# Where a load at the layer changes is placed: by loads of lead on both sides, in place of the longest idle

## The chip, the cores and the metric

The kernel runs on one NeuronCore of a Trainium2 chip. The metric is the time of one execution on the device in microseconds (us); less is better. Three runs of the kernel before took 2502.89, 2504.6 and 2510.55 us, median 2504.6.

## The reference

Two layers, each a grouped-query attention block on a cached context and then a token-mixing MLP, for two sequences with one new token each:

```python
x = A_x
x = x + _A_ref(_layernorm(x), A_k_cache, A_v_cache, A_wq, A_wo)
x = x + _B_ref(_layernorm(x), B_w1, B_b1, B_w2, B_b2)
# ... and both once more, with the same caches and weights
```

`_A_ref` makes 32 query heads from x, takes softmax(q k / sqrt(128)) v against 8 key and value heads of 32768 positions by 128, and projects back with wo. `_B_ref` normalises over the 512 channels, widens the one token to 1792 with gelu, and narrows it again. Everything is float32, and each layer reads the whole cache again: 268 MB of keys and 268 MB of values.

## The kernel before

**Units and chunks.** A unit is one (layer, sequence, key head): 2 x 2 x 8 = 32 of them, numbered 0 to 31 by the list `units`. A unit has 8 chunks of keys and 8 of values, each of 4096 positions: 2 MB, 16 KB in each of the 128 partitions. "K16 c5" below is chunk 5 of the keys of unit 16, "V15 c4" chunk 4 of the values of unit 15. For a K chunk TensorE makes scores (`k_chunk`, line 413), for a V chunk it adds weights times values (`v_chunk`, line 555). The second layer of a sequence can only begin when its first is done, so the order of units is bent at three places, N1 = 13, N2 = 16 and N3 = 18: there the last unit of one layer runs into the first of the next, and the mixer runs between. Of head 7 (the keeper), some chunks stay on the chip from layer 0 to layer 1 and aren't loaded again: three K chunks (`KEPT_K`, in cells 0, 1 and 9) and seven V chunks in whole or in part (`KEPT`, in cells 6, 2, 11, 13, 3, 4, 5 for chunks 1 to 7).

**Steps.** All chunks of K and V stand in one list, `stream`, in the order in which TensorE takes them. A step t is a place in that list, counted in chunks; it runs from 0 to 511. The loop at the end of the kernel walks through the list: for each entry it issues the load and then the matmuls. All loads of K, V and weights are issued by SyncE (SP) on one queue, in this order (line 139); SP waits at each until the place it goes to has been read for the last time. Since SP isn't held up by TensorE otherwise, it runs ahead of the matmuls as far as free places allow, and so many loads stand in the queue.

**Places.** `mem` is one tile of SBUF: cells 0 to 8 of 2 MB form the ring for chunks, cells 9 to 12 are for weights (9 and 11 also take chunks), and behind them is a rest where part of V c4 stays. A half cell is 1 MB: "7.0" and "7.5" are the halves of cell 7. Away from the changes, loads are of 2 or 4 chunks and take cells in turn (`buffer`). At the changes (units 13 to 19, steps 216 to 311) they are of one chunk and go through `spread`, which returns one whole cell or two halves, or, for the rest of a partly kept V chunk, through `half`.

**The books of the planner**, all in Python, at build time:

- `busy`: for each half cell, the step by which its content has been read; for a whole cell the first half counts half a step earlier.
- `loaded`: chunks' worth of loads issued so far; `seen[t]`: that number at step t.
- `lead(k)`: the loads issued since the last use of place k. It says how much stands in the queue between the moment the place comes free and the load that goes there.
- `booked`: for each half cell, the steps at which a kept chunk will be loaded to it.
- `closed`: for cells 6 to 9, the step from which something else has them.

In the kernel before, `half` takes the half cell that has been idle longest among those that `clear` allows: no booked load between now and 1.5 steps after the last use. `spread` takes, of the whole cells with a lead of 2 or more that `clear` allows, the one idle longest; if there is none, two halves from `half`.

The kept V chunks of unit 16 are loaded in a changed order: `SOONER` loads V16 c1 (to cell 6) right before K16 c6 at step 259, and V16 c3 (to cell 11) before K17 c0 at step 263. For V15 c4 and V18 c4, two blocks that were kept in PSUM are copied by VectorE to the place of the chunk's rest (line 503), and the last eighth of a chunk is loaded.

Of the kernel before, what the change touches and what calls it, by code (L numbers as in the profile page):

```python
# [14 lines left out]
CK = 4096  # L15
JT = CK // P
# [8 lines left out]
KEPT_K = {0: 0, 1: 1, 2: 9}  # L25
KEPT = {1: (8, 6), 2: (4, 2), 3: (8, 11), 4: (5, 13), 5: (8, 3), 6: (8, 4), 7: (8, 5)}
# [10 lines left out]
QT = 4  # L37
# [7 lines left out]
def gqa_mixer_kernel(ctx: ExitStack, tc: tile.TileContext, x, kt, v, wqo, cols, out):  # L45
# [54 lines left out]
    WCELL0, WCELLS = RING * RING, 4  # L100
# [3 lines left out]
    mem = const.tile([P, (WCELL0 + WCELLS) * CK + REST * QT * DH], F32, name="mem")  # L104

    def cells(k, m=1):
        return mem[:, k * CK : (k + m) * CK]
# [9 lines left out]
        nc.sync.dma_start(cells(cell), wqo[h])  # L117


    HB = CK // 2  # L120
    busy = [0] * 2 * (WCELL0 + WCELLS + 1)
    now = [0]
    loaded, seen = [0], {0: 0}

    def hold(k, m, until):
        for j in range(2 * k, 2 * (k + m)):
            busy[j] = max(busy[j], until - 0.5 * (m == 1 and j == 2 * k))

    def idle(k, m=1):

        return max(busy[2 * k : 2 * (k + m)])

    def lead(k, m=1):

        t = idle(k, m)
        return loaded[0] - seen[-(-t // 1)] + (-t) % 1

    def load(t, src):
        nc.sync.dma_start(t, src)  # L139
# [2 lines left out]
    def buffer(m, limit, until):  # L142

        ks = range(0, limit - m + 1, m) if limit != EVEN else [k + j for k in PAIRS for j in range(0, 2, m)]
        k = min(ks, key=lambda k: idle(k, m))
        assert idle(k, m) <= now[0]
        hold(k, m, until)
        return cells(k, m)

    def half(until):  # L150

        k = min((j for j in range(2 * WCELL0) if clear(j, until)), key=lambda j: busy[j])
        assert busy[k] <= now[0]
        busy[k] = until
        return mem[:, k * HB : (k + 1) * HB]

    def clear(k, until):

        return until <= closed.get(k // 2, until) and all(r <= now[0] or r >= until + 1.5 for r in booked.get(k, ()))

    def spread(until):

        whole = [k for k in (*range(WCELL0 + 1), KEPT[3][1]) if idle(k) <= now[0] and lead(k) >= 2 and clear(2 * k, until) and clear(2 * k + 1, until)]
        if whole:
            k = min(whole, key=idle)
            hold(k, 1, until)
            return [cells(k)]
        return [half(until - 0.5), half(until)]
# [6 lines left out]
    booked, closed = {}, {}  # L175
# [134 lines left out]
    def unit_of(n):  # L310

        return units[n]
# [67 lines left out]
    def load_k(n, c, m, limit):  # L380
        layer, b, h = unit_of(n)
        stay = h == keeper and c in KEPT_K
        own = KEPT_K[c] if stay else None
        until = k_done[n, c + m - 1]
        if own is not None:
            if stay and not layer:
                until = k_done[units.index((1, b, h)), c + m - 1]
            hold(own, m, until)
            bufs = [cells(own, m)]
        elif limit == RING:  # L390
            bufs = spread(until)
        else:
            bufs = [buffer(m, limit, until)]
        src, f = piece(kt, b * HKV + h, c, m), 0
        for t in bufs:
            if not (stay and layer):
                load(t, src[:, f : f + t.shape[-1]])
            f += t.shape[-1]
        at = [q for t in bufs for q in quads(t)]
        for j in range(m):  # L400
            k_at[n, c + j] = at[j * (JT // QT) : (j + 1) * (JT // QT)]

    def k_chunk(n, c):

        kc = k_at.pop((n, c))
        half, i = divmod(c, PACK)
        if i == 0:
            sc_ps[n, half] = pscore.tile([P, 512], F32, name="scores")
        for k in range(SUB):
            at = R * (SUB * i + k)  # L410
            q = qpad[n % 2][:, 28 - at : 60 - at]
            for g in range(NG):
                nc.tensor.matmul(  # L413
                    sc_ps[n, half][32 * g : 32 * g + 32, :],
                    q,
                    kc[k * NG + g],
                    start=(i == 0 and k == 0),
                    stop=(i == PACK - 1 and k == SUB - 1),
                )
        if i == PACK - 1:  # L420
            if half == 0:
                mx[n] = field(n, 0, HALVES)
            nc.vector.tensor_reduce(mx[n][:, half : half + 1], sc_ps[n, half], axis=AX.X, op=ALU.max)  # L423
# [20 lines left out]
    def turn_scores(n, half):  # L444
        nc.vector.transpose(S[half], sc_ps[n, half])  # L445
# [27 lines left out]
    def stays(n, c):  # L473

        quads, cell = KEPT.get(c, (0, 0)) if unit_of(n)[2] == keeper else (0, 0)
        return quads, mem[:, cell * CK : cell * CK + quads * QT * DH]

    def load_v(n, c, m, limit):
# [7 lines left out]
        if stay:  # L486
            if layer == 0:
                load(own, src[:, :f])
                for j in range(2 if stay > QT else 1):
                    busy[2 * KEPT[c][1] + j] = v_done[units.index((1, b, h)), c]  # L490
            if stay == JT // QT:
                v_at[n, c] = at
                return
            bufs = [half(until)[:, : CK - f]]
        elif limit == RING:
            bufs = spread(until)
        else:
            bufs = [buffer(m, limit, until)]
# [319 lines left out]
    for n in range(NU):  # L818
        stream += [(n * NCH + c + m - 1, 0, n, c, m, limit) for c, m, limit in parts(n, 0)]
        for c, m, limit in parts(n, 1):  # L820
            if n in (N1, N2):
                key = (n + 1) * NCH + 1 + (c + 1) / (2 * NCH)
            elif n in (N1 + 1, N2 + 1):
                key = (n + 1) * NCH - 0.5 + max(c / (2 * NCH) - 0.5, c - ASIDE + 1)
            else:
                key = (n + 1) * NCH + c + m - 1 + (LAG if N1 < n <= N3 else 0)
# [1 line left out]
    stream.sort()  # L828


    kbeg, k_done, vbeg, v_done, t = {}, {}, {}, {}, 0
    for _, is_v, n, c, m, _ in stream:
        (vbeg if is_v else kbeg).setdefault(n, t)
        for j in range(m):
            t += 1
            (v_done if is_v else k_done)[n, c + j] = t
# [9 lines left out]
    for n in range(NU):  # L846
        layer, b, h = unit_of(n)
        kend, vend = k_done[n, NCH - 1], v_done[n, NCH - 1]
        ahead = v_done[n - 1, NCH - 1] if n else 0
# [52 lines left out]
        if units[n] == lay[layer, b][-1]:  # L902
            key = (layer, b)
# [53 lines left out]
    t = 0  # L957
# [69 lines left out]
```

## Time and profile before

| | |
|---|---|
| median of three runs | 2504.6 us (2502.89 to 2510.55) |
| the profiled execution | 2504.29 us, of which the span of its instructions is 2502.5 us |
| TensorE matmuls, weight loads | busy 1391.0 us (56%), 376.7 us (15%) |
| VectorE, ScalarE, GpSimd | busy 222.8, 185.3, 4.9 us |
| read from HBM | 1063.81 MB |
| mean granted TensorE clock | 0.774 |

How to read the views of the profile: a row of the timeline has start, duration, engine and line, what it writes and reads, the count, and in brackets the idle time before it and who ended it. In a row of the windows view the last three numbers are the granted TensorE clock, the busy share of the 16 DMA engines and GB/s. A row of the chain (the work that ended last, followed back from the end) has start, duration and what; a DMA in it lasts from its issue to its landing, so it contains the time for which it stood in the queue. "SPq" is an instruction of SP's queue.

### The profile page before, as it was taken

How to read it: one execution, taken by the hardware profiler on the slowest of the kernel's cores; microseconds unless marked ns; L12 is line 12 of the kernel's file. 1: busy time of each engine (PE TensorE's matmuls, PEld its weight loads, DVE VectorE, ACT ScalarE, POOL GpSimd, SP SyncE). 2: the span in 40 equal slices, each digit the busy share in tenths (PEclk: the TensorE clock that was granted, in tenths of full speed). 3: DMA queues.
4: the chain of work that ended last, by engine and by line, in shares of the span. 5: the costliest groups of instructions: out<-in, count | busy, mean ns of one | idle time of the engine just before them, and what ended most of it. 6: DMA issues, size and time to landing. Idle time of an engine off the chain costs nothing.

```text
span 2502.5 us, 20559 instructions
## 1 busy us (share of the span) xinstructions
PE 1391.0 (56%) x9326; PEld 376.7 (15%) x9326; DVE 222.8 (9%) x610; ACT 185.3 (7%) x550; POOL 4.9 (0%) x17
## 2 busy tenths in 40 slices
PE   4545554645445544667667875455546555455546
PEld 1111111111111111111111211111111111111112
DVE  0000000000000000001111110000000000010002
ACT  0000000000000000001002010000000000012002
POOL 0000000000000000000000000000000000000000
PEclk8777777777777777878888888677777677777878
DMA  9999999999999999999999999999999999999996
GB/s 419 434 434 432 435 429 434 431 435 432 431 430 431 433 432 432 428 425 413 426 381 423 423 431 433 430 432 433 433 430 432 433 436 432 430 435 428 432 433 288
DMA packets 34368, 1065.14 MB, mean 426 GB/s; under 512 B 4069, under 2 KB 4073, under 8 KB 4970
## 3 DMA queue, kind: packets, MB, share of 16 engines
q1 hardware_dynamic: 33992, 1063.80, 98.9%
q8 instruction: 73, 1.20, 0.2%
q14 instruction: 13, 0.11, 0.0%
q10 hardware_dynamic: 290, 0.04, 0.0%
HBM read 1063.81 MB, written 0.00 MB: 425 GB/s over the span
## 4 chain that ended last, share of the span: by engine, by line
DMA 72%; PE 26%; DVE 1%; issue 0%; ACT 0%; SPq 0%; POOL 0%; ACTq 0%; DVEq 0%
DMA mem<-in_v_dram 36%; DMA mem<-in_kt_dram 36%; PE scores L413 12%; PE acc L555 11%; PE kept L337 1%; PE rows L235 1%; PE bcast L337 1%; PE small L592 0%; PE small L349 0%; PE small L439 0%; ACT S L777 0%; PE small L584 0%; PE bcast L789 0%; PE kept L734 0%; SPq L139 0%
## 5 line engine op out<-in xcount | busy, mean ns | idle before, releaser
L413 PE MATMUL scores<-mem,small_sb 128*32 128x512 f32 x4096 | 637.1, 735 | 603.6 <-DMA mem<-in_kt_dram 602.9
L555 PE MATMUL acc<-mem,S 128*16 128x512 f32 x4088 | 608.4, 731 | 451.3 <-DMA mem<-in_v_dram 442.6
L413 PEld LDWEIGHTS scores<-mem,small_sb 128*32 128x32 f32 x4096 | 152.6, 128 | 987.5 <-issue 906.3
L450 ACT ACTIVATE S<-S,small_sb 128x128 f32<-128x128 f32 x240 | 123.4, 518 | 2101.9 <-DVE small_sb L441 1632.4
L555 PEld LDWEIGHTS acc<-mem,S 128*16 128x16 f32 x4088 | 134.0, 110 | 808.3 <-issue 682.0
L423 DVE TENSOR_REDUCE small_sb<-scores 128x1 f32<-128x512 f32 x64 | 44.3, 691 | 882.0 <-PE scores L413 882.0
L445 DVE STREAM_TRANSPOSE S<-scores 128x512 f32<-128x512 f32 x64 | 45.5, 710 | 126.2 <-PE acc L555 126.2
L337 PE MATMUL kept<-mem,small_sb 128*2 128x512 f32 x104 | 51.6, 622 | 1.7 <-DVE small_sb L263 1.7
L235 PE MATMUL rows<-mem,small_sb 128*1 128x512 f32 (+1 forms) x276 | 48.9, 621 | 3.1 <-ACT mem L777 2.4
L450 ACT ACTIVATION_READ_ACCUMULATOR S<-S,small_sb 128x1 f32 x240 | 44.8, 187 | 0.0
L435 DVE TENSOR_REDUCE small_sb<-small 1x4 f32<-1x128 f32 x32 | 8.8, 276 | 284.2 <-PE small L433 284.2
L525 DVE SCALAR_TENSOR_TENSOR S<-acc,small_sb,S 128x128 f32<-128x128 f32 x93 | 32.6, 351 | 3.3
L586 DVE RECIPROCAL small_sb<-small 128x4 f32<-128x4 f32 x32 | 5.9, 185 | 280.8 <-PE small L584 280.8
L594 DVE TENSOR_TENSOR small_sb<-small,small_sb 128x4 f32<-128x4 f32 x31 | 5.1, 164 | 284.8 <-PE small L592 284.8
L777 ACT ACTIVATE S<-bcast,small_sb 128x512 f32<-128x512 f32 x28 | 20.7, 775 | 97.7 <-DVE small_sb L646 83.9
L235 PE MATMUL rows<-S,small_sb 128*1 128x512 f32 (+1 forms) x56 | 21.1, 592 | 8.0 <-ACT S L777 8.0
L349 PE MATMUL small<-small_sb,mem 2*128 2x2 f32 x112 | 15.1, 252 | 17.9 <-DVE mem L346 17.9
L523 DVE TENSOR_SCALAR S<-acc,small_sb 128x128 f32<-128x128 f32 x31 | 10.9, 350 | 139.1 <-PE acc L555 139.1
L592 PEld LDWEIGHTS small<-small_sb,S 128*128 128x128 f32 x62 | 12.5, 252 | 49.1 <-issue 38.9
L337 PE MATMUL bcast<-mem,small_sb 128*1 128x512 f32 (+1 forms) x40 | 18.5, 592 | 1.2 <-DVE small_sb L306 1.2
L349 PEld LDWEIGHTS small<-small_sb,mem 2*128 2x128 f32 x112 | 13.9, 191 | 30.8 <-DVE mem L346 27.6
L592 PE MATMUL small<-small_sb,S 128*128 128x4 f32 x62 | 15.2, 316 | 5.0 <-DVE S L525 5.0
(132 smaller groups left out, 270.5 us busy)
## 6 DMA issues: line engine op xcount, KB each, us to landing
mem<-in_kt_dram SPq DMA_DIRECT2D x35, 2048.0 KB, 17.5
mem<-in_v_dram SPq DMA_DIRECT2D x20, 2048.0 KB, 15.7
mem<-in_v_dram SPq DMA_DIRECT2D x9, 4096.0 KB, 29.1
mem<-in_v_dram SPq DMA_DIRECT2D x29, 1024.0 KB, 10.6
mem<-in_wqo_dram SPq DMA_DIRECT2D x14, 2048.0 KB, 33.4
mem<-in_kt_dram SPq DMA_DIRECT2D x7, 4096.0 KB, 25.5
mem<-in_kt_dram SPq DMA_DIRECT2D x18, 1024.0 KB, 8.9
mem<-in_v_dram SPq DMA_DIRECT2D x2, 1280.0 KB, 15.4
```

The costliest lines, as they stand in the source:

```text
L235: nc.tensor.matmul(rows[32 * g : 32 * g + b + 1, :], weights if b else weights[:, 1:], row, start=False, stop=True, skip_group_check=True,)
L337: nc.tensor.matmul(q_ps[n][:m, :], xnT[:, d, b : b + m], wq_at(h)[:, d, :], start=(d == 0), stop=(d == DT - 1),)
L349: nc.tensor.matmul(pt[:, r * m : (r + 1) * m], q_row[n][:m, r * DH : (r + 1) * DH], ident[:m, :m], start=True, stop=True,)
L413: nc.tensor.matmul(sc_ps[n, half][32 * g : 32 * g + 32, :], q, kc[k * NG + g], start=(i == 0 and k == 0), stop=(i == PACK - 1 and k == SUB ...
L423: nc.vector.tensor_reduce(mx[n][:, half : half + 1], sc_ps[n, half], axis=AX.X, op=ALU.max)
L445: nc.vector.transpose(S[half], sc_ps[n, half])
L450: nc.scalar.activation(s[:, :, h], s[:, :, h], AF.Exp, bias=neg[n][:, h : h + 1], scale=SCALE, accum_out=lsum[n][:, half, h : h + 1],)
L523: nc.vector.tensor_scalar_mul(t, acc[:, :DH], mask[:, 0:1])
L525: nc.vector.scalar_tensor_tensor(t, acc[:, k * DH : (k + 1) * DH], mask[:, k : k + 1], t, op0=ALU.mult, op1=ALU.add)
L555: nc.tensor.matmul(acc[32 * g : 32 * g + R * QT, :], S[half][:, col : col + R * QT], vc[q], start=(c == 0 and q < NG), stop=(c == NCH - 1 ...
L592: nc.tensor.matmul(po[:, :R], asb, selh, start=True, stop=True)
L777: nc.scalar.activation(hid[key, f], px[key], AF.Gelu_apprx_tanh, bias=shift[key][:, f : f + 1], scale=slope[key][:, f : f + 1],)
```

## The change

A place now has a mark, `fit`, from which both `half` and `spread` choose. It is the least of: the lead of the place; for each booked load that is still to come, the loads between the new content's last use and that step (`between`, from a new list `brings` that holds for each step what it brings, so that kept chunks count nothing); 4; and 0 where the place is closed too early. A place still in use has lead 0. The highest mark wins, and among equal ones the longest idle. `spread` takes a whole cell if its mark is 2 or more, and else two halves. `clear` is gone. `hold` and `idle` take half cells too.

```diff
     def lead(k, m=1):
         t = idle(k, m)
-        return loaded[0] - seen[-(-t // 1)] + (-t) % 1
+        return loaded[0] - seen[-(-t // 1)] + (-t) % 1 if t <= now[0] else 0
...
     def half(until):
-        k = min((j for j in range(2 * WCELL0) if clear(j, until)), key=lambda j: busy[j])
-        assert busy[k] <= now[0]
-        busy[k] = until
-        return mem[:, k * HB : (k + 1) * HB]
-
-    def clear(k, until):
-        return until <= closed.get(k // 2, until) and all(r <= now[0] or r >= until + 1.5 for r in booked.get(k, ()))
+        k = min((k / 2 for k in range(2 * WCELL0)), key=lambda k: (-fit(k, 0.5, until), idle(k, 0.5)))
+        assert fit(k, 0.5, until) >= 1
+        hold(k, 0.5, until)
+        return mem[:, int(k * CK) :][:, : CK // 2]
+
+    def fit(k, m, until):
+        ahead = [between(until, r) for j in range(int(2 * k), int(2 * (k + m))) for r in booked.get(j, ()) if r > now[0]]
+        return min(4, lead(k, m), *ahead, 0 if until > closed.get(int(k), until) else 4)
+
+    def between(a, b):
+        return sum(brings[int(-(-a // 1)) : b])

     def spread(until):
-        whole = [k for k in (*range(WCELL0 + 1), KEPT[3][1]) if idle(k) <= now[0] and lead(k) >= 2 and clear(2 * k, until) and clear(2 * k + 1, until)]
-        if whole:
-            k = min(whole, key=idle)
+        k = min((*range(WCELL0 + 1), KEPT[3][1]), key=lambda k: (-fit(k, 1, until), idle(k)))
+        if fit(k, 1, until) >= 2:
             hold(k, 1, until)
             return [cells(k)]
         return [half(until - 0.5), half(until)]
...
-    kbeg, k_done, vbeg, v_done, t = {}, {}, {}, {}, 0
+    kbeg, k_done, vbeg, v_done, brings, t = {}, {}, {}, {}, [], 0
     for _, is_v, n, c, m, _ in stream:
+        kept_k = unit_of(n)[2] == keeper and c in KEPT_K
+        brings += m * [1 - (stays(n, c)[0] / (JT // QT) if is_v else kept_k) * unit_of(n)[0]]
```

More of the change, by code (lines that the diff above doesn't have):

```diff
@@ L117, in load_weights @@
         nc.sync.dma_start(cells(cell), wqo[h])
-    HB = CK // 2
     busy = [0] * 2 * (WCELL0 + WCELLS + 1)
@@ L125, in hold @@
     def hold(k, m, until):
-        for j in range(2 * k, 2 * (k + m)):
+        for j in range(int(2 * k), int(2 * (k + m))):
             busy[j] = max(busy[j], until - 0.5 * (m == 1 and j == 2 * k))
     def idle(k, m=1):
-        return max(busy[2 * k : 2 * (k + m)])
+        return max(busy[int(2 * k) : int(2 * (k + m))])
     def lead(k, m=1):
         t = idle(k, m)
-        return loaded[0] - seen[-(-t // 1)] + (-t) % 1
+        return loaded[0] - seen[-(-t // 1)] + (-t) % 1 if t <= now[0] else 0
     def load(t, src):
```

## Prediction

> **What bounds the kernel now.** I read the page first, then the windows around the changes, then the chain and SP's timeline where the windows show a hole. From the page:
>
> ```profile
> span 2502.5 us, 20559 instructions
> ...
> q1 hardware_dynamic: 33992, 1063.80, 98.9%
> ...
> DMA 72%; PE 26%; DVE 1%; issue 0%; ACT 0%; SPq 0%; POOL 0%; ACTq 0%; DVEq 0%
> ```
>
> The loads' packets take 98.9% of what sixteen DMA engines have in the span: the kernel is bound by loading, and the change moves no byte. So it can only win what the queue stands idle, and only lose by letting it stand idle elsewhere. Where does it stand idle? Windows (the last two columns are DMA share and GB/s):
>
> ```profile
> 1100.00:1130.00 30.00, 20.11 (x124) 4.08 (x118) 3.72 (x11) 5.78 (x18) 0.00 (x0) 0.83 1.01 427
> ...
> 1250.00:1265.00 15.00, 10.25 (x72) 2.69 (x72) 1.14 (x4) 4.15 (x16) 0.00 (x0) 0.77 1.01 429
> 1265.00:1270.00 5.00, 2.20 (x24) 0.35 (x12) 1.89 (x3) 0.00 (x0) 0.00 (x0) 1.00 0.97 408
> 1270.00:1275.00 5.00, 4.24 (x24) 1.35 (x28) 0.00 (x0) 0.00 (x0) 0.00 (x0) 0.66 0.69 280
> 1275.00:1280.00 5.00, 5.00 (x34) 1.29 (x27) 0.00 (x0) 0.00 (x0) 0.00 (x0) 1.00 0.27 61
> 1280.00:1285.00 5.00, 3.90 (x27) 1.51 (x25) 1.46 (x3) 0.00 (x0) 0.00 (x0) 1.00 0.87 367
> 1285.00:1310.00 25.00, 13.89 (x92) 3.52 (x96) 1.29 (x4) 0.29 (x1) 0.00 (x0) 0.73 1.01 429
> 1360.00:1390.00 30.00, 25.00 (x142) 6.97 (x142) 6.47 (x15) 7.74 (x10) 0.55 (x1) 0.94 1.01 420
> 1430.00:1460.00 30.00, 20.22 (x126) 4.40 (x126) 2.42 (x8) 4.15 (x16) 0.00 (x0) 0.80 1.01 427
> 1460.00:1490.00 30.00, 22.19 (x156) 6.12 (x160) 3.49 (x7) 0.00 (x0) 0.00 (x0) 0.83 1.02 430
> ```
>
> There is one hole in the stretch. Against 429 GB/s it costs 5 us times (1-408/429) + (1-280/429) + (1-61/429) + (1-367/429), that is 0.24 + 1.74 + 4.29 + 0.72 = **7.0 us**. What opens it stands in SP's timeline and the chain:
>
> ```profile
> 1256.62 8.40 SPq L139 DMA_DIRECT2D mem<-in_kt_dram  x3
> 1265.53 13.51 SPq L139 DMA_DIRECT2D mem<-in_v_dram  x2
> 1279.13 0.86 SPq L139 DMA_DIRECT2D mem<-in_kt_dram  x2
> ```
>
> ```profile
> 1198.78 15.30 DMA mem<-in_v_dram
> ...
> 1216.10 17.57 DMA mem<-in_kt_dram
> ...
> 1237.38 10.96 DMA mem<-in_kt_dram
> ...
> 1256.62 14.01 DMA mem<-in_kt_dram
> ...
> 1277.77 0.92 PE scores L413 x3
> ...
> 1278.71 0.33 SPq L139
> ...
> 1279.13 11.61 DMA mem<-in_kt_dram
> ```
>
> The three K issues from 1256.62 are K16 c4 and the two halves of c5; the two V issues are V15 c4's rest (1265.53) and V16 c1, which goes at 1278.71, released by scores. V16 c1 belongs in cell 6, and the code before put the first half of K16 c5 into 6.0, two chunks earlier: it lands, is multiplied, and only then may V16 c1 be issued, with an eighth of a load between.
>
> Two constants follow. V14 c6 lands at 1198.78 + 15.30 = 1214.08 and K16 c1, seven loads later, at 1237.38 + 10.96 = 1248.34: **4.89 us a load**. From an empty queue V16 c1 and K16 c6 landed 1278.71 to 1279.13 + 11.61 = 1290.74, 12.03 us for two: a start of **2.25 us**, so a lone load needs 7.14 from issue to landing, a half 4.7.
>
> **The change part by part.** I applied the new mark by hand to each placement from step 216 to 311, with the busy steps of the code before. As a sample, K16 c5 at step 257: 251.5 loads are issued. 6.0 has lead 2.5, but until its booked load at 259 there comes only V15 c4's eighth: mark 0.125. 7.0 was last used at 253.5, when 250 had been issued: 1.5 + 0.5, mark 2. 7.0 wins, then 7.5 with 1.5. The places that differ (before, then after):
>
> | step, load | before | after |
> |---|---|---|
> | 220, 222: rests of V13 c2, c4 | 4.0, 5.0 | 5.0, 2.5 |
> | 257: K16 c5 | 6.0 + 7.0 | 7.0 + 7.5 |
> | 258: V15 c4 rest | 7.5 | 2.0 |
> | 259, 261: K16 c6, c7 | 2, 8 | 8, 7 |
> | 263, 265: K17 c0, c1 | 7, 2 | 2, 8 |
> | 268 to 299: cells 7 and 8 | as in the kernel before | exchanged |
> | 303, 305: K19 c4, c5 | 8, 1 | 1, 0.0 + 0.5 |
> | 306: V18 c4 rest | 0.0 | 2.0 |
> | 307: K19 c6 | 2 | 2.5 + 1.0 |
>
> *Steps 220, 222.* A wait goes, hidden as the first window shows (share 1.01). SP's waits from 1000 to 1600 us:
>
> ```profile
> SPq L139 <- DVE kept L514: 11.0, 2, 9.7
> ```
>
> The 9.7 us are V13 c7, to cell 5, behind the copy out of 5.0. It is then released by step 220, but the queue was full: **0**. What hides it are the loads in front; without them up to 9.7 us would show.
>
> *Steps 257 to 265.* TensorE in that stretch:
>
> ```profile
> 1261.86 1.91 PE L555 MATMUL acc<-mem,S 128*16 128x512 f32 x16
> 1263.58 1.90 PE L413 MATMUL scores<-mem,small_sb 128*32 128x512 f32 x16
> 1265.30 1.90 PE L555 MATMUL acc<-mem,S 128*16 128x512 f32 x16
> 1270.76 3.15 PE L413 MATMUL scores<-mem,small_sb 128*32 128x512 f32 x16 [3.56 <-DMA mem<-in_kt_dram]
> ...
> 1277.21 2.28 PE L413 MATMUL scores<-mem,small_sb 128*32 128x512 f32 x13
> ```
>
> These are steps 252 to 255 and most of 257. Now K16 c5's halves wait for step 253 (by 1265.5), V15 c4's rest for step 254, whose last matmul ends 1267.20 (a wait that is added; behind it on SP stands V16 c1, which needs step 252 alone). So V16 c1 is issued by about 1267.6 instead of 1278.71. K16 c4 landed at 1256.62 + 14.01 = 1270.63; c5 follows at 1275.5, the rest, an eighth, at 1276.1, and V16 c1 at **1281.0** instead of 1290.74 - 4.89 = 1285.85. The queue doesn't run dry. What is late next: K16 c6 waits for step 255 (1273.91) and must go by 1285.9 - 7.14 = 1278.8, 4.9 us to spare; K16 c7 for step 257 (1279.5) and must go by 1290.8 - 7.14 = 1283.7, 4.2 to spare.
>
> So the last engine's landing gains 1285.85 - 1281.0 = 4.8 us, and the bytes gain 7.0. They differ since engines run dry at different times: in the DMA view of 1256 to 1296, in slices of 1 us, the rate falls over five slices before it is 0:
>
> ```profile
> GB/s 459 377 434 434 401 426 475 385 475 410 410 410 410 401 434 383 305 193 86 41 0 0 0 262 98 426 492 344 475 459 360 492 426 377 508 377 426 508 311 475
> ```
>
> The engines that were ahead lose that lead in the hole; whether it counts at the end depends on whether it would be there without the hole. I take the middle, **-5.9**, ends -4.8 and -7.0. The Trainium skill (DMA: Bandwidth & Descriptors, section "Why a DMA increments its semaphore by 16 and not by 1") says that the engines of a transfer finish independently and that only the full count means landed; the five falling slices agree, and by that rule alone one would take the 4.8.
>
> *Cells 7 and 8 exchanged*: the same waits under other names, 0.
>
> *Steps 303 to 309.* Here waits get longer, since cells 6 to 9 are closed and the mark shrinks from 3.5 to 2.5 (c4) and to 2 and 1.5 (c5). SP, TensorE, and a row of the chain:
>
> ```profile
> 1449.09 6.19 SPq L139 DMA_DIRECT2D mem<-in_kt_dram  x2
> ...
> 1469.48 9.29 SPq L139 DMA_DIRECT2D mem<-in_kt_dram  x3
> ```
>
> ```profile
> 1451.73 3.18 PE L555 MATMUL acc<-mem,S 128*16 128x512 f32 x16 [2.40 <-ACT S L450]
> ...
> 1460.14 1.92 PE L413 MATMUL scores<-mem,small_sb 128*32 128x512 f32 x16 [0.65 <-DMA mem<-in_kt_dram]
> 1461.88 1.04 PE L555 MATMUL acc<-mem,S 128*16 128x512 f32 x8
> 1467.52 1.91 PE L555 MATMUL acc<-mem,S 128*16 128x512 f32 x8 [4.60 <-DMA mem<-in_v_dram]
> 1472.50 3.64 PE L413 MATMUL scores<-mem,small_sb 128*32 128x512 f32 x16 [3.08 <-DMA mem<-in_kt_dram]
> 1475.88 2.03 PE L555 MATMUL acc<-mem,S 128*16 128x512 f32 x16
> ```
>
> ```profile
> 1449.09 23.27 DMA mem<-in_kt_dram
> ```
>
> The PE rows are steps 298, 301, 302 (in two halves), 303, 304. K19 c4, issued at 1449.09, now waits for step 298, 1454.91; it lands at 1472.36, so it may go as late as 1465. c5's halves wait for step 301 (by 1462.1) instead of 1454.96; they land at 1474.8 and 1477.3 and must go 4.7 before. V18 c4's rest waits for the first half of step 302 (1462.9). c6's first half waits for the second half of step 302 (1469.43, must go by 1475.7), its second half for 1.0 in step 303: 1474.3 by its first half, 1476.14 at the worst, and must go by 1482.8 - 4.7 = 1478.1. **2.0 us to spare**, the least of all; c7 then waits for step 304 as before (2.7 to spare). So no hole. Two loads are split: where halves run in rows, 1360 to 1390, the rate is 420 against 427, 0.08 us for each 2 MB, **+0.2** for two; the other end is 2.25 for each load more, 4.5. I take the former: it is the row in which halves run.
>
> Sum: -5.9 + 0.2 = -5.7. On the profiled execution's 2504.29 us (span 2502.5 and 1.8 around it; 0.3 under the median shown), **2498.6 us**, 0.23% faster.
>
> **The rivals.** A difference of 0.3%, 7.5 us, is about what a measurement of this kernel can tell from no change.
>
> *The hole only moves.* K16 c6 and c7 now sit on cells read at steps 255 and 257; if step 257 ends over 4.2 us later than it did, the queue runs dry there. For it: rows of 3.64 us for a step stand beside rows of 1.90, so TensorE is not always quick. Against: step 257 waits for nothing new. All given back: 2504.3.
>
> *The placement isn't as I worked it out*, or cell 6 is still taken: 2504.3.
>
> *Slower: holes at unit 19.* c5 and c6 now go 6 to 7 us later, with 2.0 us to spare at 1.0. If TensorE reaches steps 301 to 303 more than 2 us later against the landings than before, the queue runs dry at c6, from about 6 at c5 too; two holes of the measured 7.0 give -5.9 + 14.0 = +8.1: 2512.4. Against: step 303 starts when its own load has landed, and step 301 does too.
>
> *Slower: halves don't overlap.* If each of the four halves had the start of 2.25 for itself, they would take 4 x 4.7 = 18.8 us instead of 9.8: +9.0 - 5.9 = +3.1, 2507.4. Against: the 420 GB/s where halves run in rows. The Trainium skill's page DMA: Bandwidth & Descriptors, section "Bandwidth", gives 6.15 us and 341 GB/s for a transfer of 1 MB and advises whole megabytes and more; by its figure, as an estimate, four would cost 24.6 instead of 9.8, +8.9 in all, 2513.2. The window's 420 speaks against that: that figure is of a transfer alone, and here others stand behind.
>
> **How the numbers follow.** Forecast 0.70 (own range 2497.5 to 2500), the hole moves 0.12, placement 0.06, holes at unit 19 0.07, halves 0.03; 0.02 for a gain beyond the bounds. The range takes in the bounds and the two cases at 2504.3 with some 2 us for the difference between runs: 2495 to 2507; it leaves out about 0.12. Faster by over 0.3% needs 7.5 us, past the upper bound, so only with the spread of runs: 0.13 + 0.02 = 0.15. Slower: 0.08. Within: 0.77.
>
> **What would show it.** No window of 1265 to 1285 under 400 GB/s; V16 c1 issued by about 1268, with no release by scores; in the list of issues 33 whole K loads and 22 halves instead of 35 and 18; no wait of 9.7 us on line 514; the windows from 1460 to 1490 at 420 or more. A hole there, or one shifted to 1280 to 1295, would prove me wrong.

## The result, and the profile after

The changed kernel takes 2499.15 us (median of 22 runs, 2498.28 to 2502.38), the kernel before 2504.93 (22 runs, 2502.89 to 2510.55): ratio 0.9977, 95% interval 0.997 to 0.9983, 5.8 us less. That is faster beyond doubt, but within the 0.3% that the prediction named; its 2498.6 us is 0.6 us off (5.7 us of gain forecast, 5.8 measured). The profiled execution of the changed kernel took 2501.7 us, 2.5 over its median; the last section tells why.

The windows of the changed kernel (last two columns DMA share and GB/s), where the kernel before had 408, 280, 61 and 367 GB/s from 1265 to 1285:

```profile
1265.00:1270.00 5.00, 1.73 (x18) 0.23 (x8) 1.98 (x3) 0.00 (x0) 0.00 (x0) 1.00 0.98 400
1270.00:1275.00 5.00, 4.44 (x28) 1.25 (x32) 0.00 (x0) 0.00 (x0) 0.00 (x0) 0.66 1.03 424
1275.00:1280.00 5.00, 5.00 (x34) 1.24 (x30) 0.00 (x0) 0.00 (x0) 0.00 (x0) 1.00 1.01 428
1280.00:1285.00 5.00, 3.62 (x27) 1.41 (x23) 1.46 (x3) 0.00 (x0) 0.00 (x0) 1.00 1.01 433
1285.00:1310.00 25.00, 15.44 (x118) 4.24 (x118) 3.48 (x10) 2.64 (x10) 0.00 (x0) 0.86 1.00 425
1360.00:1390.00 30.00, 25.86 (x164) 7.83 (x163) 10.44 (x22) 5.50 (x7) 0.54 (x1) 0.94 1.01 422
1430.00:1460.00 30.00, 19.96 (x126) 4.59 (x126) 2.95 (x8) 4.14 (x16) 0.00 (x0) 0.77 1.00 426
1460.00:1490.00 30.00, 24.54 (x172) 7.06 (x172) 3.92 (x9) 0.00 (x0) 0.00 (x0) 0.83 1.01 426
```

The hole is gone, and no other has opened at unit 19. SP's timeline and the chain of the changed kernel at the same place:

```profile
1257.01 8.39 SPq L138 DMA_DIRECT2D mem<-in_kt_dram  x3
1265.97 0.80 SPq L138 DMA_DIRECT2D mem<-in_v_dram  x2
1274.14 5.47 SPq L138 DMA_DIRECT2D mem<-in_kt_dram  x2
```

```profile
1257.01 13.41 DMA mem<-in_kt_dram
...
1274.14 11.71 DMA mem<-in_kt_dram
```

The two V issues, V15 c4's rest and V16 c1, now stand right behind one another, 0.80 us for both, where 13.51 lay from the first to the end of the second. V16 c1 is issued at 1266.35 and not at 1278.71. K16 c6 lands at 1274.14 + 11.71 = 1285.85; one load of 4.89 earlier, at 1280.96, V16 c1 has landed: 1281.0 was forecast. And the list of issues, with 33 whole K loads and 22 halves (35 and 18 before), answers to the placement that was worked out by hand. Followed load by load, the planner's code gives every place of the prediction's table, and one more that the table lacks: at step 218 V13 c0 goes to cell 4 and not to 11.

```profile
mem<-in_kt_dram SPq DMA_DIRECT2D x33, 2048.0 KB, 17.6
...
mem<-in_kt_dram SPq DMA_DIRECT2D x22, 1024.0 KB, 8.7
```

### The profile page after: what moved, and what is told of

The parts are those of the page before. It is cut to its first block, busy times and chain, and to the rows that moved or that the text cites. A ratio compares the mean times of both kernels' runs of the same rounds, so it can differ in the third digit from the quotient of the medians.

```text
span 2499.9 us, 20566 instructions
## 1 busy us (share of the span) xinstructions
PE 1400.0 (56%) x9326; PEld 380.2 (15%) x9326; DVE 222.9 (9%) x610; ACT 185.6 (7%) x550; POOL 4.9 (0%) x17
## 4 chain that ended last, share of the span: by engine, by line
DMA 72%; PE 26%; DVE 1%; ACT 1%; issue 0%; SPq 0%; POOL 0%; ACTq 0%
DMA mem<-in_v_dram 37%; DMA mem<-in_kt_dram 35%; PE scores L416 11%; PE acc L558 11%; PE rows L238 1%; PE kept L340 1%; PE bcast L340 0%; ACT S L780 0%; PE small L595 0%; PE small L442 0%; PE small L587 0%; PE kept L737 0%; PE small L352 0%; PE bcast L641 0%; DVE S L528 0%
## 5 line engine op out<-in xcount | busy, mean ns | idle before, releaser
L558 PE MATMUL acc<-mem,S 128*16 128x512 f32 x4088 | 615.5, 739 | 445.1 <-DMA mem<-in_v_dram 439.4
```

The lines of the kernel that those rows point to most:

```text
L558: nc.tensor.matmul(acc[32 * g : 32 * g + R * QT, :], S[half][:, col : col + R * QT], vc[q], start=(c == 0 and q < NG), stop=(c == NCH - 1 ...
```

## The experiments

Theory: all of the time is the hole in front of V16 c1, and it is as long as cell 6 stays taken. Rivals: part of the gain comes from the other changed places; the longer waits or the splits at unit 19 give part of it back. Ratios are to the kernel before, measured beside it. Their intervals reach some 0.0009 to each side, 2.3 us: the times alone tell the whole hole from none, but not 1 or 2 us of it, and for those the traces must decide.

### e1_margin: the kernel before, with one number changed

```diff
-        return until <= closed.get(k // 2, until) and all(r <= now[0] or r >= until + 1.5 for r in booked.get(k, ()))
+        return until <= closed.get(k // 2, until) and all(r <= now[0] or r >= until + 2 for r in booked.get(k, ()))
```

> The kernel before with one number changed: a place is barred when its booked load comes within 2 steps of the content's last use, not 1.5. By the planner's books that keeps K16 c5 out of cell 6 and gives the placement of the changed kernel from step 257 on, unit 19 included; steps 220 and 222 stay as before. Theory (all of the time is the hole at V16 c1): 5.8 us under the kernel before, ratio 0.9977, no window under 400 GB/s from 1265 to 1285. Rival (the earlier release of V13 c7 at steps 220 and 222 carries part of the gain): 2 to 4 us of gain, ratio 0.9984 to 0.9992.

Measured 2499.58 us, ratio 0.9979 (0.9969 to 0.9988). Its rate from 1256 to 1296 us, in slices of 1 us:

```profile
GB/s 410 459 369 442 393 475 418 434 418 459 369 434 393 426 377 442 440 447 406 428 410 475 393 426 459 426 410 426 410 459 410 426 459 410 410 475 410 426 393 426
```

No slice is near 0. The theory holds: with steps 218, 220 and 222 as they were, the medians lie 5.5 us apart, against 5.8 with the change. (The interval also takes in the rival's 0.9984; e2 tries the same steps from the other side.)

### e2_half_in_6: one placement of the changed kernel undone

```diff
         k = min((k / 2 for k in range(2 * WCELL0)), key=lambda k: (-fit(k, 0.5, until), idle(k, 0.5)))
-        assert fit(k, 0.5, until) >= 1
+        k = {257.5: 6}.get(until, k)
+        assert fit(k, 0.5, until) >= 1 or k == 6
```

> The changed kernel with one placement undone: the first half of K16 c5 goes to 6.0 again, all else by the new mark. Theory: the hole is back, V16 c1 issued at about 1278.7 after scores, ratio to the kernel before 1.0000 within 0.0005. Rival (the gain is spread over the other placements): ratio 0.9985 to 0.9995.

Measured 2504.67 us, ratio 1.0001 (0.9992 to 1.001). SP's timeline, and the rate from 1256 to 1296:

```profile
1265.55 13.78 SPq L138 DMA_DIRECT2D mem<-in_v_dram  x2
```

```profile
GB/s 459 401 410 393 410 459 418 434 467 401 410 451 369 434 401 414 354 207 94 45 0 0 0 66 229 393 393 492 377 410 492 377 442 492 377 442 475 377 459 426
```

The hole is back in the same slices, with 13.78 us for the two V issues (V16 c1 goes at 1279.01), and all of the gain is gone, though steps 218, 220 and 222 and unit 19 stand as in the changed kernel. By the planner's code the edit moves other loads up to step 270 too, K16 c6 back to cell 2 for one; the trace lays the loss on V16 c1. With e1 this settles it as far as the times reach (the interval leaves the other places 2 us at most): half a chunk in cell 6 makes the difference.

### e3_rest_in_6: cell 6 taken one step longer

```diff
-        assert fit(k, 0.5, until) >= 1
+        k = {259: 6}.get(until, k)
+        assert fit(k, 0.5, until) >= 1 or k == 6
```

> The changed kernel, but the rest of V15 c4 (step 258) goes to 6.0, so V16 c1 waits one step longer than in the kernel before. Step 258 was multiplied from 1280.2 on and 6.0 is read first, so V16 c1 goes at about 1281.5 and lands at 1288.6, 7.6 us after the 1281.0 of the changed kernel, where the kernel before lost 4.9. Theory (the loss follows the step at which the place comes free): 2.5 to 3 us slower than the kernel before, ratio 1.0010 to 1.0012. Rival (the loss is not this wait): ratio 0.9977 as with the change.

Measured 2510.14 us, ratio 1.0018 (1.0009 to 1.0027): slower, as the theory has it, by 4.5 us (0.0018 of 2505.07; 5.1 by the medians) where 2.5 to 3 was expected. The interval, 2.3 to 6.8 us, holds both, but the trace shows a later issue than I had taken. TensorE, then SP, then the rate:

```profile
1280.67 2.29 PE L559 MATMUL acc<-mem,S 128*16 128x512 f32 x13
```

```profile
1283.12 0.33 SPq L138 DMA_DIRECT2D mem<-in_v_dram  x1
```

```profile
GB/s 410 434 410 434 393 434 418 459 451 410 377 410 401 410 418 406 313 215 72 43 0 0 0 0 0 0 0 0 262 295 492 508 295 508 459 344 492 459 344 508
```

V16 c1 was issued at 1283.12, 0.16 us after the last matmul of step 258 (1280.67 + 2.29 = 1282.96). I had taken 1281.5, believing that 6.0 is read first. It is read last: five blocks of V15 c4 stay elsewhere and come first in the step (`at = at + rest` in `load_v`), and the rest comes at its end. From 1278.71 to 1283.12 are 4.4 us, and the measured 4.5 over the kernel before agree. So, within its interval, the time follows the moment of release.

### e4_no_exchange: unit 19 as before

```diff
+        k = {269: 8, 271: 8.5}.get(until, k)
         assert fit(k, 0.5, until) >= 1
```

> The changed kernel with the rests of V16 c2 and c4 in 8.0 and 8.5 as before; cells 7 and 8 are then not exchanged, and the loads of unit 19 stand as in the kernel before (K19 c4 to 8, c5 to 1, c6 to 2, none split). Theory (the splits at unit 19 cost 0.2 us and no hole): 0.2 us under the changed kernel, ratio 0.9976. Rival (the longer waits at unit 19 give back 1 to 2 us of the 7.0 that the bytes gain): ratio 0.9970 to 0.9973, faster than both.

Measured 2499.37 us, ratio 0.9977 (0.9968 to 0.9986). Its list of issues shows that nothing is split:

```profile
mem<-in_kt_dram SPq DMA_DIRECT2D x35, 2048.0 KB, 17.6
...
mem<-in_kt_dram SPq DMA_DIRECT2D x18, 1024.0 KB, 9.7
```

The rival's 1 to 2 us are not there: the medians differ by 0.2 us, and the wrong way. The interval alone would still allow them, but the landings don't: from K19 c4's to c7's there are 15.35 us in e4 and in the kernel before, where nothing is split, and 15.48 in the changed kernel. Two splits and the longer waits of unit 19 cost 0.13 us there.

### e5_split_all: what a split costs

```diff
-        nc.sync.dma_start(t, src)
+        w = CK // 2 if t.shape[-1] == CK else t.shape[-1]
+        for i in range(0, t.shape[-1], w):
+            nc.sync.dma_start(t[:, i : i + w], src[:, i : i + w])
```

> The changed kernel with each load of one whole chunk (53 of K and V) issued as two loads of 1 MB, one behind the other, to the two halves of its cell; places and waits stay. It measures what a split costs by itself. Theory (halves overlap in the queue, 0.08 us for each split): 4 us over the changed kernel at most, 2503, ratio to the kernel before 0.9977 to 0.9994. Rival (each half has the start of 2.25 us for itself): 119 us more, ratio 1.045.

Measured 2502.82 us, ratio 0.9992 (0.9983 to 1.0001). The list of issues:

```profile
mem<-in_kt_dram SPq DMA_DIRECT2D x88, 1024.0 KB, 17.9
mem<-in_v_dram SPq DMA_DIRECT2D x69, 1024.0 KB, 15.2
```

88 K and 69 V halves against 22 and 29 in the changed kernel: 106 halves more, so 53 splits. 2502.82 - 2499.15 = 3.7 us, **0.07 us a split**, where 0.08 was worked out and the rival had 2.25. (The two ratios lie 0.0015 apart, by their intervals 0.0004 to 0.0026, which leaves 0.02 to 0.12.) In a queue that holds other loads, the start of 2.25 us doesn't show.

### e6_whole_late: a mark of 1 where the change asks for 2

```diff
-        if fit(k, 1, until) >= 2:
+        if fit(k, 1, until) >= (1 if now[0] > 300 else 2):
```

> The changed kernel, but from step 300 on a whole cell is taken with a mark of 1 or more, not 2: K19 c5 goes whole to cell 0 (mark 1.5) and c6 whole to cell 1 (mark 1.125), so c6 waits for all of step 303. Theory (what decides is whether the issue is 7.14 us before the landing that is due; c6 misses that by 0.4): 0 to 1 us over the changed kernel, ratio 0.9977 to 0.9981. Rival (a mark under 2 opens a hole such as that of mark 0.125): 3 to 5 us over it, ratio 0.9989 to 0.9997.

Measured 2500.41 us, ratio 0.9984 (0.9976 to 0.9993): 1.3 us over the changed kernel by the medians, 1.8 by the ratios, so a little over the theory and under the rival. By the intervals it could be anything from no loss to some 4 us; the trace shows what happened. SP's timeline of e6, with K19 c6 at 1471.09, and its rate from 1450 to 1490:

```profile
1471.09 2.70 SPq L138 DMA_DIRECT2D mem<-in_kt_dram  x3
```

```profile
GB/s 442 377 492 393 426 475 369 385 459 385 516 393 426 492 377 426 442 393 408 283 158 41 274 393 393 492 377 442 442 410 459 426 623 524 295 295 459 508 524 492
```

From 1469 to 1473 there is a small hole: 283, 158, 41, 274. So K19 c6 came just too late, as its mark of 1.125 and the 7.14 us had it.

## Why the prediction was right

**Which hole, and which half chunk.** The prediction laid the whole gain on cell 6. e1 and e2 show it from both sides, and e3 lengthens the wait and pays for it. The waits that were said to be late next, K16 c6's and c7's, opened nothing: the windows from 1270 to 1310 stand at 424 to 433.

**How much: between the landing and the bytes.** The prediction took -5.9 as the middle of 4.8, by which the last landing moves, and 7.0, the bytes that the hole doesn't move. Measured: 5.8, by its interval 4.3 to 7.5, so the time alone doesn't tell the middle from either end. The runs gave two more holes to try that on, each against the changed kernel. By the bytes, the windows from 1265 to 1290 of the changed kernel, the kernel before and e3, then from 1465 to 1480 of the changed kernel and e6 (the first four 5 us windows above are too short for e3's hole):

```profile
1265.00:1290.00 25.00, 18.42 (x130) 5.02 (x120) 3.44 (x6) 0.00 (x0) 0.00 (x0) 0.93 1.01 423
```

```profile
1265.00:1290.00 25.00, 15.34 (x104) 4.49 (x92) 3.35 (x6) 0.00 (x0) 0.00 (x0) 0.83 0.76 308
```

```profile
1265.00:1290.00 25.00, 15.45 (x104) 4.60 (x96) 3.35 (x6) 0.00 (x0) 0.00 (x0) 0.83 0.58 233
```

```profile
1465.00:1480.00 15.00, 12.63 (x82) 3.39 (x86) 1.89 (x3) 0.00 (x0) 0.00 (x0) 0.77 1.03 423
```

```profile
1465.00:1480.00 15.00, 12.60 (x82) 3.33 (x86) 2.08 (x4) 0.00 (x0) 0.00 (x0) 0.79 0.89 358
```

By the landing, V16 c1's issue and 7.14 us, against 1280.96. For e6, K19 c6 goes at 1471.09 and lands at 1478.2; without a hole it would follow K19 c4, whose matmuls begin at 1467.40, by c5's 4.89, an eighth and its own 4.89, at about 1477.6:

```profile
1467.40 3.64 PE L416 MATMUL scores<-mem,small_sb 128*32 128x512 f32 x16 [3.07 <-DMA mem<-in_kt_dram]
```

| hole | last landing | bytes | measured, by ratios |
|---|---|---|---|
| kernel before | 4.9 | 25 x (1 - 308/423) = 6.8 | 0.0023 x 2504.93 = 5.8 |
| e3 | 1283.12 + 7.14 - 1280.96 = 9.3 | 25 x (1 - 233/423) = 11.2 | 0.0041 x 2505.07 = 10.3 (medians 11.0) |
| e6 | 0.6 | 15 x (1 - 358/423) = 2.3 | 0.0007 x 2504.43 = 1.8 (medians 1.3) |

All three lie between the columns, which are 2 us apart for a hole of any length; the intervals are too wide to say where between. What is lost beyond the landing can be seen behind the hole. Starts of V16 c0's matmuls, which wait for its landing, in the kernel before, the changed kernel and e2:

```profile
1316.76 3.61 PE L555 MATMUL acc<-mem,S 128*16 128x512 f32 x16 [2.81 <-DMA mem<-in_v_dram]
```

```profile
1310.57 2.87 PE L558 MATMUL acc<-mem,S 128*16 128x512 f32 x16 [1.95 <-DMA mem<-in_v_dram]
```

```profile
1317.03 1.91 PE L559 MATMUL acc<-mem,S 128*16 128x512 f32 x16 [2.77 <-DMA mem<-in_v_dram]
```

The difference was 4.9 us at V16 c1 and is 6.2 six loads later, with the queue full in between; for e2 it goes from 5.2 to 6.5.

The traces also hold the sixteen increments of each load's semaphore, one for the share of each engine, and there the cause can be read. Of V15 c4's rest, the last load ahead of the hole in the kernel before, the first share landed 3.75 us ahead of the last, and the mean share 2.2; of V16 c1, behind the hole, 0.40 and 0.2. So the engines come out of the hole in step, and the lead that is gone, 2.0 us in the mean, is what the bytes count more than the landing. The next four loads land 4.9 us apart. Then K17 c1 takes 6.24, its last share 1.34 behind the second last: one engine has fallen back, and the whole load waits for it. e2 and e3 have the same at K17 c1 (6.23 and 6.16), and e6 has it at the second load behind K19 c6, with a last share 1.37 behind the others. In the changed kernel the first and the last share stay 3.6 to 3.7 us apart. There one of the shares that were 1.4 us ahead of the last falls back by 1.1 between K17 c1 and V16 c0, but it had that lead to lose, and the landing moves by 0.13.

So the loss was the landing and then one late engine, 4.9 + 1.3 = 6.2 in the trace, and the prediction named the right thing, a lead that is lost, without knowing how much of it would count. That the middle came so close is luck: of 2.0 us of lead, a late engine happened to cost 1.3. What makes an engine fall back stays open; no run tried it. The rule of the Trainium skill that engines finish independently (DMA: Bandwidth & Descriptors, "Why a DMA increments its semaphore by 16 and not by 1") agrees with the shares 3.75 us apart and with the five falling slices; 4.8 alone, which I drew from it, leaves the late engine out.

A lower rate is not a loss by itself. The prediction speaks of one hole, but its windows leave out this one of the kernel before:

```profile
1150.00:1155.00 5.00, 4.91 (x30) 0.93 (x22) 1.39 (x6) 0.00 (x0) 0.55 (x1) 0.81 0.87 333
```

The changed kernel has 315 GB/s there. Only engines that were ahead stood idle: the shares of a load go from 5.5 us apart to 3.2, and the last ones still land 2.5 us apart, as those of halves do elsewhere.

**Steps 220 and 222: 0.** Step 218, which the prediction left out, belongs to them; it cost nothing either. SP's waits from 1000 to 1600 us have no 9.7 on that copy any more. One of 6.3 remains, K14 c4's first half, which now has 2.5 behind V13 c4's rest:

```profile
SPq L138 <- DVE kept L517: 7.6, 2, 6.3
```

The rate from 1100 to 1130 was 427 GB/s before and stays so; e1, which has V13 c0 in cell 11 and the wait of 9.7 still, is as quick within its interval.

**Unit 19: +0.2 and no hole.** The time of e4 can't tell it from 0, the landings make it 0.13, and e5 puts a split at 0.07 instead of 0.08. Halves were said to have 2.0 us to spare at worst, and no hole opened; e6 takes whole cells with less, and a hole of 0.6 us by the landing opens, where 0.4 was worked out.

**The rival of single transfers** fell: e5 shows 0.07 us where the Trainium skill's figure for 1 MB (same page, "Bandwidth", 6.15 us) would, as an estimate, make 7.4 more for each split, 6.15 x 2 - 4.89. The page's transfers were issued from GpSimd, those here from SP, with others in the queue.

## What to carry to other kernels

In a kernel bound by loading, look for the windows in which the DMA rate falls, ask whether the landings behind them are late, and read from SP's timeline which single load was: here 5.8 us hung on one half chunk that had been put, two steps before V16 c1 was due, into the cell promised to it. A planner of buffers does well to weigh what comes between the last use of a place and its next load on both sides, in loads; what must be kept is the time from issue to landing from an empty queue (7.14 us here, some one and a half loads). Splitting a load to get a place with more lead was nearly free as long as the queue wasn't empty (0.07 us). And here a barring margin raised from 1.5 to 2 steps, with the longest idle place chosen as before, did as much as the new mark.

## What the runs showed of the hardware that was not expected

The tail has two lengths. From the last landing to the end there were 16.3 us in the kernel before (2458.23 + 27.94 = 2486.17, span 2502.5) and 18.3 in the changed kernel (2451.40 + 30.17 = 2481.57, span 2499.9). The chains:

```profile
2458.23 27.94 DMA mem<-in_v_dram
```

```profile
2451.40 30.17 DMA mem<-in_v_dram
```

The 5 us behind the last landing, in the kernel before, in the changed kernel, and in e1, whose last landing at 2452.05 + 27.95 = 2480.00 leaves 16.5 us to its span of 2496.5:

```profile
2486.20:2491.20 5.00, 4.17 (x40) 2.66 (x40) 2.52 (x9) 0.38 (x1) 0.26 (x1) 1.00 0.00 0
```

```profile
2481.60:2486.60 5.00, 4.68 (x32) 2.56 (x33) 1.14 (x4) 0.38 (x1) 0.00 (x0) 0.55 0.00 0
```

```profile
2480.00:2485.00 5.00, 4.17 (x40) 2.66 (x40) 2.50 (x9) 0.39 (x1) 0.23 (x1) 1.00 0.00 0
```

The granted clock (third number from the end) was 0.55 in the changed kernel's and 1.00 in the others', so its last matmuls, which nothing hides, took longer (eight of one shape 1.03 us against 0.61), and the tail 2 us. In the other traces with the short tail, e2 to e5, it is 16.4 to 16.5 us, at a clock of 1.00. A late engine comes on top: of the changed kernel's last load but one, the last share landed 1.52 us behind the second last, and 1.35 remain at the last load. The two together, some 3.3 us, are why the spans differ by 2.6 us where the medians differ by 5.8, and more than the 2.5 us by which that execution lies over its median. e4's, also 2.5 over its median, has the short tail, but a late engine of 2.3 us. The profiled execution of e6, 3.5 us over its median, had both, a late engine of 2.05 us and the long tail, behind a last landing at 2454.06 + 29.96 = 2484.02:

```profile
2484.00:2489.00 5.00, 4.57 (x32) 2.47 (x33) 1.17 (x4) 0.38 (x1) 0.00 (x0) 0.60 0.00 0
```

Its clock was 0.60 there, and its tail 18.1 us (span 2502.1). The medians of 10 runs and more are what the comparisons above rest on.
